# Attention's first two units in another order of issue, and copies of row maxima placed behind the exponentials

## The chip, the core and the metric

The kernel runs on one NeuronCore of a Trainium2 chip, in one launch. The metric is the device time of that launch in microseconds (us); lower is better. The engines are named as the profile names them: PE is TensorE (matmuls), DVE is VectorE, ACT is ScalarE, POOL is GpSimd, SP is SyncE, whose queue here only issues DMAs. Each engine runs its own instructions in the order in which the program holds them, and waits at an instruction whose inputs are not there.

## What is computed

Three layers follow each other: causal attention with a cumulative decay, a mixture of experts, and a gated two-layer net with a short convolution. The change touches the first alone:

```python
B, H, S, D = 4, 8, 576, 64
scores = q @ k.transpose(0, 1, 3, 2) / np.sqrt(D)
cum = np.cumsum(np.maximum(s, 0.0), axis=-1)
bias = -(cum[:, :, :, None] - cum[:, :, None, :])
scores = np.where(causal, -1000000000.0, scores + np.minimum(bias, 0.0))
scores = scores - np.max(scores, axis=-1, keepdims=True)
attn = np.exp(scores)
attn = attn / (np.sum(attn, axis=-1, keepdims=True) + 1e-09)
out = np.matmul(attn, v)
```

## The kernel before

The 32 pairs of batch and head are worked in eight units of four heads each; unit u is half of batch u // 2. A sequence has 576 = 512 + 64 positions; the last 64, the tail, are kept for all heads together in the buffers T1 and T2.

**Operands.** q and k of a unit are loaded as float32 (`load`, L164), scaled and split into two float16 numbers, a high and a low one: ScalarE writes the high part (`split_hi`, L258), VectorE (units 0 and 1) or GpSimd (units 2 to 7) subtracts it from the number to get the low part (`split_lo`, L265). Both parts are then transposed, so that the head dimension lies on partitions: for unit 0 and the tail by matmuls with a unit matrix (`turned`, L299), for the other units by DMA transposes that SyncE issues (`turn`, L278). The result is U[u, 2] (k2 in the program); `copy` (L287) brings its high part into U[u, 1], one of three buffers K1 that the units take in turn. The rows above row 63 of K1 hold what is added to the scores: rows 64 to 69 the decay in three float16 numbers (`extra`, for unit 0 `extra_first`, for the tail `extra_tail`), row 127 of the q half the maximum of the row. For that, the unit's scores are computed once ahead in float16 (`stage_a`: 14 pieces, unit 0 has 15, into PSUM tiles za), VectorE reduces each piece to its maxima (L389, L417), TensorE turns the maxima into rows (`max_turn`, L454), ScalarE copies them out of PSUM (`max_out`, L459; tile mr), and a DMA of `max_row` (L466, for the tail L469) writes them into row 127. Only then may the unit's scores proper start, since they subtract the maximum within the matmul.

**Steps.** A step is one PSUM tile z of 512 scores: `scores` (L488, L491, L516) at step t, the exponentials on ScalarE (`weights`, L527, L532, L533) one step later, the low part on VectorE (`rest`, L544) two steps later, the product with v (`values`, L560) four steps later. A unit has 14 steps. Everything else is placed by hand: a task is planned at a step, with a fraction that orders the tasks of one step, and `work(t)` issues them ahead of the step's scores. The tables in PAR hold these places; those of `start` below zero are issued ahead of step 0. So what matters is the order on each engine:

```python
plan(t0 + c["mx"] + 1, lambda u=u: max_turn(u))
plan(t0 + c["mx"] + 1, lambda u=u: max_out(u))
plan(t0 + c["mx"] + 2, lambda u=u: max_row(u))
```

**SyncE's queue** carries nearly all loads, transposes and rows in one order. With unit 1's row 127 the order is: unit 1's four transposes (two of k, two of q), its decay rows (`extra`), a block of zeros for the output, k and q of unit 3 (L169), k of unit 4 into the buffer that unit 2's k has left, the second half of the first batch's v (L179, L183), unit 2's two transposes, its decay rows, and unit 1's row of maxima. Names of `start` that the steps speak of: `ldq1`, `lk2`, `lq2` are loads; `hk1`, `hq1`, `lk1`, `lq1` the splits of unit 1; `tlk`, `tlq` those of the tail; `T1k`, `T1q` unit 1's transposes; `x1` its decay rows; `xt` the tail's; `mt..`, `mo..`, `mr..` are max_turn, max_out and max_row of unit 0's halves (a, b) and of the tail (t); `pa` to `pd` and `pt` its pieces; `sv0` the split of v.

Of the kernel before, what the change touches and what calls it, by code (L numbers as in the profile page):

```python
# [9 lines left out]
F32 = mybir.dt.float32  # L10
# [16 lines left out]
NH = 4  # L27
# [18 lines left out]
class Keep:  # L46
# [6 lines left out]
PAR = {'u1': {'sv': -3, 'pa': -6, 'pn': 4, 'mx': -3},  # L53
 'u2': {'at': (-22, -21, -19, -18.9, -18), 'cp': (-14, -13), 'lv': -11, 'sv': -2, 'pa': -12, 'pn': 7, 'mx': -6},
# [25 lines left out]
           'wm': -28,  # L80
           'pa': -27,
# [3 lines left out]
           'ldq1': -23,  # L85
           'pb': -22,
           'pc': -21,
           'pd': -20,
           'mtb': -19,
           'thq': -18,  # L90
           'hk1': -17,
           'mob': -16,
           'mrb': -15,
           'lk2': -14,
           'lq2': -13,
           'tlk': -12,
           'tlq': -11,
           'lk1': -10,
           'xt': -9,
           'T1k': -8,  # L100
           'ttk': 2.0,
           'ttq': 3.0,
           'hq1': 3.05,
           'lq1': 3.06,
           'T1q': 3.07,
           'x1': 3.08,
           'ct': 4.0,
           'pt': 4.1,
           'c2': 4.5,
           'sv0': 4.6,  # L110
           'mtt': 5.0,
           'mot': 5.1,
           'mrt': 5.2,
           'z': 6.0,
           'lv1': 8.5},
# [8 lines left out]
def attention(tc, ctx, q, k, v, s, xd, rt, hook):  # L124
# [140 lines left out]
    def split_lo(u, n):  # L265
        i = AT[n]
        a, h = U[u, n].rearrange("p h c (t d) -> p (h c t) d", t=2), U[u, "h"][:, i]
        if u < 2:
            V.scalar_tensor_tensor(h[:, :, i], in0=a, scalar=scale[n], in1=h[:, :, 1 - i], op0=ALU.mult, op1=ALU.subtract)
        else:  # L270
            G.tensor_scalar(a, a, scale[n], 0.0, op0=ALU.mult, op1=ALU.add)
            G.tensor_tensor(h[:, :, i], a, h[:, :, 1 - i], op=ALU.subtract)
# [47 lines left out]
    def extra_first(j):  # L320
        for r, n in ((64, 0), (67, 1)):
            for e in range(2):
                Q.dma_start(K1[0][r + j:r + j + 1, e, n].rearrange("o (h c) -> o h c", h=NH), cp[0:NH, j, 256 * e:256 * e + 256])
# [5 lines left out]
    def copy_tail():  # L329
        for i in range(2):  # L330
            V.tensor_copy(T1[0:64, :, i], T2[64 - 64 * i:128 - 64 * i, :, i])
# [44 lines left out]
    def stage_a(u, halves=False):  # L376
# [14 lines left out]
        def piece(i, hs):  # L391

            n, m = 128 * i + 128, len(hs)
            z = aps.tile([128, 512], F32, name="za")
# [61 lines left out]
    def max_out(u, hs=slice(0, 4), tails=True):  # L456
        n = span(hs, tails).stop - span(hs, tails).start
        mr = U[u, "mr", key(hs)] = wk.tile([18, 128], F16, name="mr")
        A.activation(mr[0:n], U[u, "mt"][0:n, 0:128], AF.Copy, scale=2.0 ** -12)  # L459
# [201 lines left out]
    todo, pieces, copies = {}, {}, {6: [(1, "k")], 7: [(1, "q")]}  # L661

    def plan(t, f):
        todo.setdefault(math.floor(t), []).append((t, len(todo), f))

    def work(t):
        for x in sorted(todo.get(t, ()), key=lambda x: x[0]):
            x[2]()
# [9 lines left out]
    def second_a(r):  # L678
# [12 lines left out]
        xt=extra_tail, ct=copy_tail, ldq1=lambda: load(1, "q"), lk2=lambda: load(2, "k"), lq2=lambda: load(2, "q"),  # L691
# [14 lines left out]
    for u in range(1, NU):  # L706
# [17 lines left out]
        plan(t0 + c["mx"] + 1, lambda u=u: max_out(u))  # L724
# [4 lines left out]
    for t in range(N + 9):  # L729
# [5 lines left out]
        work(t)  # L735
# [9 lines left out]
        if at(2):  # L745
            rest(at(2))
        for d, f in ((4, values), (5, norm), (6, xout)):
            y = at(d)
            if y and y[2] == (3 if y[1] % 2 else 2):
                f(y[0], y[1])  # L750
# [761 lines left out]
def attn_moe_moe2(tc, q, k, v, s, wg, wl, w1, w2, w_in, conv, w_out, out):  # L1512
    nc = tc.nc
    w_in, conv, w_out = (t.bitcast(I32) for t in (w_in, conv, w_out))
    with tc.manual_schedule(), ExitStack() as ctx:
# [13 lines left out]
        def hook(t):  # L1529
# [17 lines left out]
            if PAR["h"]["rc"] <= t < PAR["h"]["rc"] + 80:  # L1547
                for x in range(PAR["h"]["rk"] if t > PAR["h"]["rc"] else 1):
                    next(lay.steps[0], None)
                if t >= PAR["h"]["rc"] + 3:  # L1550
                    next(lay.steps[1], None)
# [98 lines left out]
```

## Time and profile before

| what | us |
|---|---|
| median of three runs | 699.95 |
| lowest and highest of the three | 696.01, 701.78 |
| the profiled execution | 697.92 |
| its span, first to last instruction | 696.2 |
| busy in that span: PE, DVE, ACT, POOL | 631.4, 447.4, 390.6, 250.6 |

The profile is of one execution. Its timeline lists instructions by start, in us from the start of the span, with their duration; equal ones that follow each other are put together with a count. In brackets stands the idle time of the engine ahead of an instruction and what ended it. A list of waits adds such idle times up. The granted clock is a share of TensorE's full 2.4 GHz.

### The profile page before, as it was taken

To read this page: it belongs to the slowest core of one execution; us is meant where nothing else is said; L and a number is where in the kernel's file an instruction comes from. 1 tells how busy PE (TensorE), PEld (TensorE's weight loads), DVE (VectorE), ACT (ScalarE), POOL (GpSimd) and SP (SyncE) were. 2 spreads that over 40 slices of the span, in tenths; PEclk is the share of its full clock that TensorE was granted. 3 is DMA by queue.
4 is the path that set the end of the run, shared out by engine and by line. 5 is a ranking of instruction groups with operands and counts; after the bars stand their busy time and mean duration, and the time that the engine had idled before them with its cause. 6 is when DMAs were issued, how large, how long until landed. Compare 5 with 4: busy or idle time off the path is not lost. (4 is left out here: it accounts for less than half of the span.)

```text
span 696.2 us, 15401 instructions
## 1 busy us (share of the span) xinstructions
PE 631.4 (91%) x5176; PEld 393.5 (57%) x5176; DVE 447.4 (64%) x860; ACT 390.6 (56%) x660; POOL 250.6 (36%) x363
## 2 busy tenths in 40 slices
PE   5675989899999579989999999999599999999997
PEld 2344778688888434434444444444277766665443
DVE  6876688988866696585768586662049984645000
ACT  5553677787788737474746373532059974545111
POOL 8658866654441059812634434342100000000000
PEclk9988899999999769999999999999799999999999
DMA  5876886756646446999999999762390210000111
GB/s 123 189 165 94 145 168 106 169 100 117 183 157 209 129 163 166 296 313 280 248 344 233 325 186 252 180 156 64 69 167 6 46 40 31 16 31 31 45 52 54
DMA packets 168827, 101.81 MB, mean 146 GB/s; under 512 B 119712, under 2 KB 147016, under 8 KB 168732
## 3 DMA queue, kind: packets, MB, share of 16 engines
q1 hardware_dynamic: 164744, 88.65, 53.0%
q0 software_dynamic: 3984, 11.99, 5.5%
q8 instruction: 47, 0.77, 0.5%
q14 instruction: 48, 0.39, 0.2%
q10 hardware_dynamic: 4, 0.00, 0.0%
HBM read 62.18 MB, written 15.31 MB: 111 GB/s over the span
## 5 line engine op out<-in xcount | busy, mean ns | idle before, releaser
L1216 PE MATMUL hp<-r,xt 128*128 x504 | 113.9, 383 | 4.9 <-ACT xt L1247 4.9
L1216 PE MATMUL yp<-r,ht 128*128 x504 | 112.2, 379 | 1.3 <-PEq L1329 1.3
L1484 PE MATMUL o<-wo,g 128*128 128x512 f16 x432 | 94.5, 379 | 0.0
L1436 PEld LDWEIGHTS <-wi 128*128 128x128 f16 x768 | 76.2, 99 | 25.7 <-SPq L1403 4.1
L1216 PEld LDWEIGHTS <-xt 128*128 128x128 f16 x504 | 49.5, 99 | 65.6 <-ACT xt L1247 6.5
L1216 PEld LDWEIGHTS <-ht 128*128 128x128 f16 x504 | 48.5, 98 | 57.0 <-issue 2.3
L1158 DVE SCALAR_TENSOR_TENSOR r<-st,r 128x512 f32 (+3 forms) x80 | 68.3, 914 | 8.8 <-ACT r L1147 7.0
L1436 PE MATMUL hp<-yt,wi 128*128 128x288 f16 x576 | 71.9, 286 | 0.0
L1484 PEld LDWEIGHTS <-g 128*128 128x128 f16 x432 | 42.3, 98 | 49.5
L1147 ACT ACTIVATE r<-st 128x512 f32 (+3 forms) x84 | 57.4, 761 | 21.5 <-SPq L1209 14.6
L1279 POOL DMA_INDIRECT yd<-ys,idx x21 | 21.9, 1041 | 127.1 <-DVEq L1200 63.8
L389 DVE TENSOR_REDUCE mx<-za 128x1 f32<-128x384 f32 (+4 forms) x97 | 56.8, 602 | 14.4 <-PE za L386 13.6
L532 ACT ACTIVATE phi<-z,lnes 128x512 f16<-128x512 f32 (+1 forms) x80 | 50.6, 633 | 24.5 <-PE z L491 22.1
L488 PE MATMUL z<-k 128*128 128x128 f16 (+2 forms) x320 | 50.2, 281 | 9.7 <-DMA k<-mr 5.9
L544 DVE TENSOR_TENSOR plo<-z,phi 128x512 f16<-128x512 f32 (+1 forms) x80 | 48.2, 603 | 13.4 <-ACT z L533 8.7
L533 ACT ACTIVATE z<-z,lnes 128x512 f32<-128x512 f32 (+1 forms) x80 | 48.6, 607 | 0.0
L1453 DVE SCALAR_TENSOR_TENSOR c<-hb,cw,c 128x576 f32<-128x576 f32 x32 | 26.1, 815 | 34.6 <-ACT c L1447 34.6
L1487 ACT ACTIVATE s<-o 128x512 f32<-128x512 f32 x18 | 10.7, 597 | 61.5 <-PE o L1484 61.4
L560 PE MATMUL o<-v,p 128*128 128x65 f32 x256 | 45.0, 287 | 0.0
L1441 ACT ACTIVATE hb<-hp 128x576 f32<-128x576 f32 x32 | 20.5, 642 | 37.9 <-PE hp L1436 37.9
L560 PE MATMUL o<-vv,phi 128*128 128x65 f16 (+1 forms) x512 | 41.6, 202 | 0.0
L1277 ACT ACTIVATE ys<-yp,pp 128x512 f16<-128x512 f32 x21 | 14.3, 683 | 48.4 <-PE yp L1216 34.7
(291 smaller groups left out, 1224.6 us busy)
## 6 DMA issues: line engine op xcount, KB each, us to landing
st<-in_moe_w_dram SPq DMA_DIRECT2D x8, 2048.0 KB
st<-in_moe_w_dram SPq DMA_DIRECT2D x24, 512.0 KB
out_dram<-s SPq DMA_DIRECT2D x18, 256.0 KB
st<-in_k_dram SPq DMA_DIRECT2D x16, 256.0 KB
st<-in_q_dram SPq DMA_DIRECT2D x16, 256.0 KB
xd<-xh SPq DMA_DIRECT2D x16, 256.0 KB
k<-in_moe_w_dram SPq DMA_DIRECT2D x8, 512.0 KB
s<-in_moe_w_in_dram SPq DMA_DIRECT2D x16, 256.0 KB
```

Of the source, the lines that this page charges most:

```text
L389: return lambda: V.tensor_reduce(out, z.rearrange("p (e c) -> p e c", e=m), axis=AX.X, op=ALU.max)
L488: PE.matmul(out, lhsT=ks[i], rhs=qs[i], start=first and not i, stop=False, skip_group_check=True)
L532: A.activation(hi[:, 0:n], z[:, 0:n], AF.Exp, bias=lnes, scale=1.0 / SC)
L533: A.activation(p[:, 0:n], z[:, 0:n], AF.Exp, bias=lnes, scale=1.0 / SC)
L544: (V if md == "a" else G).tensor_tensor(lo[:, 0:n], p[:, 0:n], hi[:, 0:n], op=ALU.subtract)
L560: PE.matmul(out, lhsT=w, rhs=x, start=first, stop=last, skip_group_check=True)
L1147: i = self.nc.scalar.activation(hi, src, AF.Copy, scale=self.scale[w])
L1158: i = nc.vector.scalar_tensor_tensor(lo, in0=src, scalar=sc, in1=hi, op0=ALU.mult, op1=ALU.subtract)
L1216: i = self.nc.tensor.matmul(out, lhsT=lhsT, rhs=self.rings[w][:, c, k, bass.ds(s, 1), f], **kw)
L1436: PE.matmul(st[x][:, n, 0:HN], lhsT=wi[:, c, k, m], rhs=t[:, n, a + k], start=k + a + c == 0, stop=k == 3 and a == 4)
L1453: V.scalar_tensor_tensor(c, in0=h[:, 1:S + 1], scalar=cw[:, m, 1:2], in1=c, op0=ALU.mult, op1=ALU.add)
L1484: PE.matmul(o, lhsT=g[:, a, k, 128 * i:128 * i + 128], rhs=wo[:, c, k], start=j == 0, stop=j == 23)
```

## The change

It has five parts. (1) The start: the last four of the twelve DMAs that write unit 0's decay rows go to GpSimd's queue; the loads of unit 1's q and the tail's decay rows come sooner on SyncE; the subtraction of unit 1's q goes from VectorE to GpSimd; the tail's two copies are made one by VectorE and one by ScalarE, each as soon as its half is turned; unit 0's last two pieces of maxima, their transpose and row go behind the first scores. (2) Every third piece of unit 0's maxima takes its PSUM tile from the pool of z. (3) Unit 1's operands and pieces come one step sooner (`copies`, `pa`, `mx`), and so do unit 2's splits. (4) `work` is called twice a step: tasks with a fraction above 0.75 are issued behind the step's scores, exponentials and subtraction; `max_out` of units 1 to 7 is among these. (5) The splits of the router's weights (L1550) start six steps later. The order of what SyncE issues from unit 1's transposes on is not changed.

The diff, without the table of the start, whose effect the rows of the orders below show:

```diff
@@ -50,8 +50,8 @@
 
 
 
-PAR = {'u1': {'sv': -3, 'pa': -6, 'pn': 4, 'mx': -3},
- 'u2': {'at': (-22, -21, -19, -18.9, -18), 'cp': (-14, -13), 'lv': -11, 'sv': -2, 'pa': -12, 'pn': 7, 'mx': -6},
+PAR = {'u1': {'sv': -3, 'pa': -7, 'pn': 4, 'mx': -4},
+ 'u2': {'at': (-22.5, -21.5, -19, -18.9, -18), 'cp': (-14, -13), 'lv': -11, 'sv': -2, 'pa': -12, 'pn': 7, 'mx': -6},
  'u3': {'load': -35, 'loadq': 0, 'at': (-33, -30, -28, -27, -26.9), 'cp': (-22, -21), 'sv': -1, 'pa': -20, 'pn': 14, 'mx': -6},
  'u': {'load': -51,
        'loadq': 8,
@@ -265,7 +266,7 @@
     def split_lo(u, n):
         i = AT[n]
         a, h = U[u, n].rearrange("p h c (t d) -> p (h c t) d", t=2), U[u, "h"][:, i]
-        if u < 2:
+        if u < 2 and (u, n) != (1, "q"):
             V.scalar_tensor_tensor(h[:, :, i], in0=a, scalar=scale[n], in1=h[:, :, 1 - i], op0=ALU.mult, op1=ALU.subtract)
         else:
             G.tensor_scalar(a, a, scale[n], 0.0, op0=ALU.mult, op1=ALU.add)
@@ -320,15 +321,19 @@
     def extra_first(j):
         for r, n in ((64, 0), (67, 1)):
             for e in range(2):
-                Q.dma_start(K1[0][r + j:r + j + 1, e, n].rearrange("o (h c) -> o h c", h=NH), cp[0:NH, j, 256 * e:256 * e + 256])
+                (G if j == 2 else Q).dma_start(K1[0][r + j:r + j + 1, e, n].rearrange("o (h c) -> o h c", h=NH), cp[0:NH, j, 256 * e:256 * e + 256])
 
     def extra_tail():
         for r, i in ((64, 0), (67, 1)):
             Q.dma_start(T1[r:r + 3, :, i], ext.rearrange("j (b h) c -> j b (h c)", b=B))
 
-    def copy_tail():
-        for i in range(2):
-            V.tensor_copy(T1[0:64, :, i], T2[64 - 64 * i:128 - 64 * i, :, i])
+    def copy_tail(n):
+        i = AT[n]
+        t = T1[0:64, :, i], T2[64 - 64 * i:128 - 64 * i, :, i]
+        if n == "k":
+            V.tensor_copy(*t)
+        else:
+            A.activation(*t, AF.Copy)
 
     def split_v(u):
         b, o = u // 2, u % 2 * NH
@@ -391,7 +396,8 @@
         def piece(i, hs):
 
             n, m = 128 * i + 128, len(hs)
-            z = aps.tile([128, 512], F32, name="za")
+            third = halves and (hs[0] // 2 * 6 + (i if i < 2 else 2 * i - 2 + hs[0] % 2)) % 3 == 2
+            z = zps.tile([128, 512], F32, name="z") if third else aps.tile([128, 512], F32, name="za")
             if halves:
                 busy(z, 1)
             for x, h in enumerate(hs):
@@ -658,14 +664,15 @@
     copy(0, "q")
     load_tail("q")
     load(1, "k")
-    todo, pieces, copies = {}, {}, {6: [(1, "k")], 7: [(1, "q")]}
+    todo, pieces, copies = {}, {}, {5: [(1, "k")], 6: [(1, "q")]}
 
     def plan(t, f):
         todo.setdefault(math.floor(t), []).append((t, len(todo), f))
 
-    def work(t):
+    def work(t, end=None):
         for x in sorted(todo.get(t, ()), key=lambda x: x[0]):
-            x[2]()
+            if end in (None, x[0] - t > 0.75):
+                x[2]()
 
     first, second = slice(0, 2), slice(2, 4)
     P0 = []
@@ -688,7 +695,7 @@
         ttk=lambda: turn_tail("k", range(4), "AVAV"), ttq=lambda: turn_tail("q", range(4), "AVAV"),
         pb=lambda: second_a(range(6, 8)), pc=lambda: second_a(range(8, 10)), pd=lambda: second_a(range(10, 12)),
         mtb=lambda: max_turn(0, second, False), mob=lambda: max_out(0, second, False), mrb=lambda: max_row(0, second, False),
-        xt=extra_tail, ct=copy_tail, ldq1=lambda: load(1, "q"), lk2=lambda: load(2, "k"), lq2=lambda: load(2, "q"),
+        xt=extra_tail, ctk=lambda: copy_tail("k"), ctq=lambda: copy_tail("q"), ldq1=lambda: load(1, "q"), lk2=lambda: load(2, "k"), lq2=lambda: load(2, "q"),
         T1k=lambda: [turn(1, e, slice(0, 1)) for e in range(2)], T1q=lambda: [turn(1, e, slice(1, 2)) for e in range(2)], x1=lambda: extra(1),
         pt=lambda: second_a(range(12, 15)), mtt=lambda: max_turn(0, None), mot=lambda: max_out(0, None), mrt=lambda: max_row(0, None),
         sv0=lambda: split_v(0), lv1=lambda: loadv(0, 1),
@@ -721,7 +728,7 @@
         for i in range(14):
             pieces.setdefault(t0 + c["pa"] + i * c["pn"] // 14, []).append((u, i))
         plan(t0 + c["mx"] + 1, lambda u=u: max_turn(u))
-        plan(t0 + c["mx"] + 1, lambda u=u: max_out(u))
+        plan(t0 + c["mx"] + 1.9, lambda u=u: max_out(u))
         plan(t0 + c["mx"] + 2, lambda u=u: max_row(u))
     for t in sorted(x for x in todo if x < 0):
         work(t)
@@ -732,7 +739,7 @@
         for f in am:
             f()
         am = []
-        work(t)
+        work(t, False)
         at = lambda d: steps[t - d] if 0 <= t - d < N else None
         if at(0):
             scores(at(0))
@@ -744,6 +751,7 @@
             weights(at(1))
         if at(2):
             rest(at(2))
+        work(t, True)
         for d, f in ((4, values), (5, norm), (6, xout)):
             y = at(d)
             if y and y[2] == (3 if y[1] % 2 else 2):
@@ -1547,7 +1555,7 @@
             if PAR["h"]["rc"] <= t < PAR["h"]["rc"] + 80:
                 for x in range(PAR["h"]["rk"] if t > PAR["h"]["rc"] else 1):
                     next(lay.steps[0], None)
-                if t >= PAR["h"]["rc"] + 3:
+                if t >= PAR["h"]["rc"] + 9:
                     next(lay.steps[1], None)
             for i in range(4):
                 if t == PAR["h"]["e"][i]:
```

The places where the order moves, line numbers being those of each kernel (before / after: L169 / L170, L281 / L282, L323 / L324, L466 / L472).

SyncE from the decay rows of unit 0 (`k_141<-cp`) to unit 1's transposes. `in_k`, `in_q` are the loads of the tail's halves (32x8x128), then of units 1 and 2; `k_141<-mr` are unit 0's two rows of maxima; `t_144<-ext` the tail's decay rows. Before:

```order
L323 DMA k_141<-cp 1x4x256 x12
L197 DMA k_146<-in_q_dram 32x8x128 x4
L169 DMA st_112<-in_k_dram 128x4x128 x2
L466 DMA k_141<-mr 1x4x128 x2
L169 DMA st_112<-in_q_dram 128x4x128 x2
L466 DMA k_141<-mr 1x4x128 x2
L169 DMA st_111<-in_k_dram 128x4x128 x2
L169 DMA st_112<-in_q_dram 128x4x128 x2
L327 DMA t_144<-ext 3x4x512 x2
L281 DMA_TRANSPOSE k_436<-st_111 128x16x64 x4
```

After:

```order
L324 DMA k_141<-cp 1x4x256 x8
L198 DMA k_146<-in_q_dram 32x8x128 x4
L170 DMA st_112<-in_k_dram 128x4x128 x2
L170 DMA st_112<-in_q_dram 128x4x128 x2
L472 DMA k_141<-mr 1x4x128 x2
L328 DMA t_144<-ext 3x4x512 x2
L170 DMA st_111<-in_k_dram 128x4x128 x2
L170 DMA st_112<-in_q_dram 128x4x128 x2
L472 DMA k_141<-mr 1x4x128 x2
L282 DMA_TRANSPOSE k_480<-st_111 128x16x64 x4
```

Four DMAs are gone from this queue, unit 1's q load and the tail's decay rows have moved up, and the second row of maxima stands right ahead of the transposes.

GpSimd, from the loads of v on; `st_112`, `st_111` and `h` are q or k of units 1 and 2 and their split halves, `k_143` the buffer K1 of unit 2. Before:

```order
L179 DMA nv<-in_v_dram 64x4x64 x8
L183 DMA nvt<-in_v_dram 32x2x64 x4
L209 MEMSET k_143 128x2x512
L209 MEMSET k_143 64x2x512
L209 MEMSET k_143 3x2x512
L341 MEMSET vv 128x16
L342 MEMSET vv 128x16
L341 MEMSET vvt 128x2
L342 MEMSET vvt 128x2
L343 MEMSET v_558 128x4
L354 TENSOR_SCALAR v_558<-nv 128x4x64
L271 TENSOR_SCALAR st_111<-st_111 128x1024
```

After:

```order
L180 DMA nv<-in_v_dram 64x4x64 x8
L184 DMA nvt<-in_v_dram 32x2x64 x4
L272 TENSOR_SCALAR st_112<-st_112 128x1024
L273 TENSOR_TENSOR st_111<-st_112,st_111 128x16x64
L210 MEMSET k_143 128x2x512
L210 MEMSET k_143 64x2x512
L210 MEMSET k_143 3x2x512
L272 TENSOR_SCALAR st_111<-st_111 128x1024
L273 TENSOR_TENSOR h<-st_111,h 128x16x64
```

The subtraction of unit 1's q (two instructions) stands ahead of the zeroing of `k_143`, and unit 2's k ahead of the small pieces of v.

ScalarE, from the copies of the turned tail on; `t_144` is T1, `p_` the weights of a step, `h<-st_111` the high part of unit 2's k, `mr` the tail's maxima. Before:

```order
L305 ACTIVATE t_145<-o 128x4x128 x2
L263 ACTIVATE st_111<-st_112 128x16x64
L527 ACTIVATE p_531<-z,lnes 128x512
L346 ACTIVATE vv<-nv 128x16x64
L346 ACTIVATE vvt<-nvt 128x2x64
L532 ACTIVATE phi<-z,lnes 128x512
L533 ACTIVATE z<-z,lnes 128x512
L459 ACTIVATE mr<-mt 2x128
L469 DMA t_144<-mr 1x2x128
L527 ACTIVATE p_595<-z,lnes 128x512
L263 ACTIVATE h<-st_111 128x16x64
```

After:

```order
L306 ACTIVATE t_145<-o 128x4x128 x2
L336 ACTIVATE t_144<-t_145 64x4x512
L533 ACTIVATE p_538<-z,lnes 128x512
L538 ACTIVATE phi<-z,lnes 128x512
L539 ACTIVATE z<-z,lnes 128x512
L264 ACTIVATE h<-st_111 128x16x64
L533 ACTIVATE p_581<-z,lnes 128x512
L351 ACTIVATE vv<-nv 128x16x64
L351 ACTIVATE vvt<-nvt 128x2x64
L465 ACTIVATE mr<-mt 2x128
```

Unit 2's k has moved ahead of the tail's row and its DMA, behind the new copy into `t_144`; the split of unit 1's q is gone from this place and stands ahead of step 0.

## Rows read from the trace of the kernel before

**Rows 1.** Waits of TensorE over the whole program: us in total, times, longest.

```profile
PE z L488 <- DMA k<-mr: 5.9, 1, 5.9
```

**Rows 2.** Timeline of TensorE, first scores of units 1 and 2.

```profile
67.86 1.01 PE L488 MATMUL z<-k 128*128 128x512 f16 x2 [5.88 <-DMA k<-mr]
...
98.40 0.59 PE L488 MATMUL z<-k 128*128 128x512 f16 x2
```

**Rows 3.** Stretches: length, busy PE, PEld, DVE, ACT, POOL, PEclk, DMA share, GB/s.

```profile
67.80:74.40 6.60, 6.54 (x52) 5.73 (x52) 2.09 (x5) 2.77 (x5) 6.36 (x10) 0.52 0.89 162
74.40:100.00 25.60, 22.08 (x309) 18.61 (x307) 22.30 (x50) 16.62 (x34) 17.37 (x52) 1.00 0.74 137
```

**Rows 4.** Timeline of SyncE's queue, 25 to 67 us: start, length of the issues.

```profile
25.55 1.20 SPq L466 DMA_DIRECT2D k<-mr  x2
...
30.66 7.53 SPq L281 DMA_TRANSPOSE k<-st  x4
...
41.84 1.08 SPq L169 DMA_DIRECT2D st<-in_q_dram  x2
45.77 1.86 SPq L169 DMA_DIRECT2D st<-in_k_dram  x2
...
55.30 8.28 SPq L281 DMA_TRANSPOSE k<-h  x2
...
65.27 1.40 SPq L466 DMA_DIRECT2D k<-mr  x2
```

**Rows 5.** Waits of SyncE's queue, 0 to 70 us.

```profile
SPq L169 <- POOL h L272: 2.8, 1, 2.8
```

**Rows 6.** Timeline of SyncE's queue, the third of unit 1's transposes.

```profile
34.15 1.90 SPq L281 DMA_TRANSPOSE k<-st  x1
```

**Rows 7.** Timeline of GpSimd, 8 to 50 us.

```profile
8.62 1.39 POOL L647 DMA_DIRECT2D ex<-cp  x2 [0.45 <-ACT cp L253]
...
18.93 4.94 POOL L179 DMA_DIRECT2D nv<-in_v_dram  x8
23.81 2.23 POOL L183 DMA_DIRECT2D nvt<-in_v_dram  x4
...
42.49 1.04 POOL L271 TENSOR_SCALAR st<-st 128x1024 f32<-128x1024 f32 x1 [12.65 <-ACT h L263]
43.62 2.12 POOL L272 TENSOR_TENSOR h<-st,h 128x1024 f16<-128x1024 f32 x1
...
47.28 2.12 POOL L272 TENSOR_TENSOR h<-st,h 128x1024 f16<-128x1024 f32 x1
```

**Rows 8.** Timeline of ScalarE, 32 to 60 us.

```profile
32.58 1.07 ACT L346 ACTIVATE vv<-nv 128x1024 f16<-128x1024 f32 x1
33.53 0.32 ACT L346 ACTIVATE vvt<-nvt 128x128 f16<-128x128 f32 x1
33.73 0.69 ACT L532 ACTIVATE phi<-z,lnes 128x512 f16<-128x512 f32 x1
...
41.36 1.05 ACT L263 ACTIVATE h<-st 128x1024 f16<-128x1024 f32 x1
...
58.88 0.27 ACT L459 ACTIVATE mr<-mt 18x128 f16<-18x128 f32 x1 [5.66 <-PE mt L454]
```

**Rows 9.** Timeline of VectorE: unit 1's subtractions, k, then q.

```profile
26.88 1.22 DVE L269 SCALAR_TENSOR_TENSOR st<-st,st 128x1024 f16<-128x1024 f32 x1
...
32.15 1.23 DVE L269 SCALAR_TENSOR_TENSOR st<-st,st 128x1024 f16<-128x1024 f32 x1
```

**Rows 10.** Timeline of SyncE's queue, 91 to 97 us: unit 2's row, a transpose.

```profile
91.60 1.50 SPq L466 DMA_DIRECT2D k<-mr  x2
...
93.79 2.91 SPq L281 DMA_TRANSPOSE k<-h  x1
```

**Rows 11.** Waits of TensorE, 70 to 215 us, the first of five.

```profile
PE za L386 <- DVE mx L389: 2.3, 4, 1.2
```

**Rows 12.** Page, costliest groups: busy, mean ns of one.

```profile
L1279 POOL DMA_INDIRECT yd<-ys,idx x21 | 21.9, 1041 | 127.1 <-DVEq L1200 63.8
```

More of the change, by code (lines that the diff above doesn't have):

```diff
@@ L80 @@
            'wm': -28,
+           'ldq1': -27.5,
            'pa': -27,
@@ L84 @@
            'mr0a': -24,
-           'ldq1': -23,
            'pb': -22,
            'pc': -21,
-           'pd': -20,
-           'mtb': -19,
            'thq': -18,
            'hk1': -17,
-           'mob': -16,
-           'mrb': -15,
+           'hq1': -16,
+           'xt': -15,
            'lk2': -14,
            'lq2': -13,
[L96 to L100, printed above, removed]
+           'pd': 1.0,
+           'mtb': 1.1,
+           'tlk': 1.2,
+           'lk1': 1.3,
+           'lq1': 1.4,
+           'tlq': 1.5,
+           'mob': 1.8,
+           'mrb': 1.9,
            'ttk': 2.0,
+           'T1k': 2.1,
+           'ctk': 2.8,
            'ttq': 3.0,
[L103 to L113, printed above, removed]
+           'T1q': 3.1,
+           'x1': 3.2,
+           'ctq': 3.3,
+           'c2': 3.5,
+           'pt': 4.8,
+           'mtt': 5.8,
+           'sv0': 5.85,
+           'mot': 5.9,
+           'mrt': 5.95,
            'z': 6.0,
-           'lv1': 8.5},
+           'lv1': 7.5},
  'r': {'cut': 12, 'w1': 6, 'w2': 8, 'w3': 5},
```

## The prediction

> **What bounds the kernel now.** I read the waits of TensorE first. The longest single one of the whole program is a wait for a DMA: matmul L488 waits 5.9 us for a row of maxima [rows 1]. The timeline of TensorE puts it at 67.86 us [rows 2]: after unit 0's last scores the engine stands idle 5.88 us, from 61.98, until unit 1's first scores may start, because row 127 of unit 1's operand has not landed. The stretch behind it runs at a granted clock of 0.52, next to the lower level of 1.2 GHz, up to 74.4 us, and from there at 1.00 [rows 3]. From 70 to 215 us the longest sum of TensorE waits is 2.3 us on VectorE, and no DMA is in that list [rows 11]: behind unit 1's start TensorE is near full, so what its start gains should stay to the end.
>
> What makes the row late is not its computation. ScalarE had copied the maxima at 58.88 + 0.27 = 59.15 us [rows 8], but SyncE issued the row at 65.27 [rows 4]. SyncE works in order and had no rest: from 45.77 it issued unit 4's k, unit 1's values, unit 2's two transposes (55.30, 8.28 us for two), unit 2's extra rows, and then the row, finished at 66.67; the first matmul came 1.19 us later. In front of 45.77 SyncE stood still from 41.84 + 1.08 = 42.92, 2.85 us, for unit 2's k to be given free: the list of SyncE's waits names GpSimd's subtraction L272 with 2.8 us [rows 5]. And in front of that it issued unit 1's four transposes, 30.66 to 38.19, the third (first of q) at 34.15 [rows 4, 6]. So unit 1's start hangs on a chain of issues, and two places in it can move: the start of unit 1's q transposes, and the 2.85 us gap.
>
> **The change part by part.** The order of SyncE's instructions behind unit 1's transposes is the same in both kernels: unit 1's row still stands behind unit 2's two transposes, whatever the change is called. Only the front is another.
>
> *Unit 1's q transposes.* Their input now needs a subtraction on GpSimd in place of one on VectorE (1.23 us at 32.15, [rows 9]). On GpSimd it stands behind the loads of v, whose last issue ended at 23.81 + 2.23 = 26.04 [rows 7], and four DMAs of the decay rows move onto that queue ahead of them. No row shows these four on GpSimd; its 12 issues of v took 4.94 + 2.23 = 7.17 us, 0.60 each, so I take 4 x 0.6 = 2.4 us (below it, nothing: the engine was waiting only 0.45 us there; above it, 1.04 us each as the indirect DMAs of L1279, [rows 12], 4.2 us). The subtraction is two instructions, 42.49 to 43.62 + 2.12 = 45.74, 3.25 us [rows 7]. So 26.04 + 2.4 + 3.25 = 31.7 us, and ScalarE's half of the split is ready well before, since the loads of unit 1's q are issued ahead of both rows of unit 0. The k transposes must be through by then: VectorE's half of k ended at 26.88 + 1.22 = 28.10 and one instruction of that size now stands behind it instead of ahead, so 26.9; the row issued ahead of them ended at 25.55 + 1.20 = 26.75 [rows 4, 9]. Two issues took 34.15 - 30.66 = 3.5 us, so they end at 30.4, in time. The q transposes start at 31.7 in place of 34.15.
>
> *A wait that is new.* The tail's extra rows now stand third behind the first row of maxima and wait for GpSimd's zeroing of that buffer, which the four DMAs push back by the same 2.4 us. Behind them queue unit 2's loads, the second row and unit 1's transposes. The zeroing ended just ahead of 18.93 [rows 7], so now at 21.4, while the second row isn't due until about 25.5: I cost it at nothing; if it is not hidden, the k transposes have 31.7 - 30.4 = 1.3 us to lose first.
>
> *The gap.* With the q transposes at 31.7, SyncE reaches unit 4's k load at 31.7 + (42.92 - 34.15 = 8.8) = 40.5. That load overwrites unit 2's k, which ScalarE splits and GpSimd then subtracts. ScalarE did its part at 41.36 to 42.41 [rows 8], behind the tail's row and its DMA; now it stands ahead of these, behind one copy that comes from VectorE, and three exponentials. The copy has 2048 elements a partition; 1024 took 1.07 and 128 took 0.32 [rows 8], 0.84 ns an element, so 1.07 + 0.86 = 1.93. VectorE's last cast that the copy needs ended by 32.15 even before [rows 9]. So 32.15 + 1.93 + 3 x 0.69 + 1.05 = 37.2, and GpSimd's 3.25 more give 40.45. The load is free as SyncE reaches it, at 40.5 in place of 45.77. The gap goes, and what is late next is SyncE's own queue.
>
> *From there to unit 1.* From 45.77 to the end of the row's issue at 66.67 were 20.9 us, then 1.19 to the matmul: 40.5 + 20.9 + 1.2 = 62.6. Two conditions lie beside it. Unit 2's transposes, now at 50.0, need data that GpSimd had ready at 47.28 + 2.12 = 49.4 even in the old order [rows 7]; the row is issued from 60.0, and ScalarE had the maxima at 59.15 even in the old order. And unit 0's work on TensorE ended at 61.98 even before. Nothing that the change does to unit 0's computation is therefore needed for the sum, and none of its gains (a third PSUM pool for every third piece of maxima, two copies and a subtraction off VectorE) counts in it: they lengthen TensorE's wait. Gain: 67.86 - 62.6 = 5.2 us.
>
> *The copies of maxima behind exponentials*, units 1 to 7: each comes at most one step's exponentials (2 x 0.69) later. Unit 2's row was issued at 91.60 + 1.50 and, at 1.2 us to land, was there at 94.3, its first scores came at 98.40 [rows 2, 10]: 4 us of room. The exponentials come sooner, but TensorE's waits in rows 11 are for VectorE. I take 0 (from a loss of nothing to a gain of 0.5 us in all).
>
> *The clock.* The idle time ahead of unit 1 shrinks but stays about as long as the distance from unit 0's new end to 62.6; the low stretch behind it stays in my sum.
>
> *Sum.* The profiled execution took 697.92 us, 1.72 more than its span of 696.2. Less 5.2 it is 692.7. The median of the three runs, 699.95, lies 2.03 above the profiled one, so the forecast for such a median is 699.95 - 5.2 = 694.7 us, its own range 693.5 to 696.5 by the pieces above.
>
> **A rule that speaks against it.** GpSimd's 12 issues of v ran at 0.60 us each [rows 7]. The Trainium skill, page "SBUF — State Buffer", section "A bandwidth-pool intuition that's wrong (but worth ruling out)", says that a DMA issued from GpSimd can take about 3.1 us in place of 0.62 when VectorE holds the port that the two share. By that figure, an estimate, four issues would cost 12.4 us, the q transposes would start at 41.7, unit 1 at 72.6, and the time would be 704.7. This trace agrees with the undisturbed figure, and shows no disturbed one. The mechanism as such is the last rival.
>
> **The rivals.** *More than the sum.* Unit 2's two transposes took 8.28 us, while a later one took 2.91 [rows 4, 10]: at 2 x 2.91 the row comes 2.5 us sooner, 7.7 in all, and should unit 0 end close to the row, the low stretch shortens too (6.6 us at 0.52 hold some 3 us). For it: the later transpose is as large. Against: unit 1's four, half as large each, took 7.53 us for the same bytes, so 8 us looks like what the DMAs need. Time: 699.95 - 7.7 = 692.3, with the clock down to 690.
>
> *Nothing moves.* If ScalarE's split of unit 2's k stays behind the tail's row (its copy waits on a later cast, or the exponentials wait on scores), GpSimd releases the buffer near 45 as before, the load goes at 45.8 and the q transposes' gain is swallowed by the gap. For it: three engines have to hand over within 0.1 us of my sum's meeting point; against it: a delay there costs only its own length, up to 5. Time: 699 to 700.
>
> *Slower: GpSimd's queue decides.* The 16 issues on GpSimd ahead of the subtraction may be dearer than 0.60 us, and unit 1's q then waits for them. Unit 1's start lies 62.6 - 31.7 = 30.9 us behind the start of the q transposes, so from 67.86 - 30.9 = 37.0 on, 5.3 us later than in my sum, the change loses. At the 1.04 us of rows 12, 16 issues cost 16.7 in place of 9.6, the subtraction ends at 38.8, unit 1 starts at 69.7: 1.8 us lost, 701.8. For it: the engine is the one with new work; against it: the 12 issues that rows 7 show.
>
> **How the numbers follow.** My forecast has a chance of 0.58, more than the sum 0.22, nothing moves 0.12, slower 0.08. The range 690.0 to 700.5 leaves out the slower rival and some of the spread of the runs, which were 696.01 to 701.78, so that 1% (7 us) is about what a measurement can tell from no change. Faster by over 1% (under 692.95): most of the second case and a sixth of the first, 0.30. Slower by over 1% (over 706.95): the dearest part of the last case, and what I have not thought of, 0.05. Within 1%: 0.65.
>
> **What would show it.** Right: in the new profile unit 1's first L488 starts near 62.6 and still waits for the row's DMA, for 3 to 5 us; the third unit 1 transpose is issued near 31.7; SyncE has no gap ahead of unit 4's k near 40.5; the end of the attention part and of the program move by the same 5 us. Wrong: the subtraction on GpSimd ends after 33; SyncE waits for GpSimd's L272 again; unit 1's wait is gone, which would say that I mis-sized unit 2's transposes; or the start comes sooner and a later stretch is longer by as much.

## The result, and the profile after

Over 15 runs of each kernel in turn the median fell from 698.03 to 691.01 us, ratio 0.9894, 95% interval 0.9872 to 0.9917: faster by 1.06%, or 7.0 us, where 5.2 us were forecast. In the profiled executions the span fell from 696.2 to 688.5 us.

The waits of TensorE, 40 to 62 us, after (in us: total, times, longest), against [rows 1]:

```profile
PE z L522 <- DMA t<-mr: 3.7, 1, 3.7
PE za L391 <- DVE k L290: 2.6, 1, 2.6
PE z L494 <- DMA k<-mr: 1.4, 1, 1.4
```

The wait for unit 1's row is down from 5.88 to 1.40 us. Two waits inside unit 0 are new or longer: for the tail's row, and for VectorE's copies. The timeline of TensorE after, first scores of units 1 and 2, and the router's first product:

```profile
61.43 0.59 PE L494 MATMUL z<-k 128*128 128x512 f16 x2 [1.40 <-DMA k<-mr]
...
89.95 0.59 PE L494 MATMUL z<-k 128*128 128x512 f16 x2
...
228.34 0.84 PE L1020 MATMUL nrp<-unit,znr 128*128 128x128 f16 x5 [1.12 <-DVE znr L998]
```

The router's first product before:

```profile
236.71 0.84 PE L1012 MATMUL nrp<-unit,znr 128*128 128x128 f16 x5 [1.12 <-DVE znr L990]
```

Against [rows 2], unit 1 starts 6.43 us sooner and unit 2 8.45. The router's product is 8.37 sooner, so units 2 to 7 are as long as they were: 236.71 - 98.40 = 138.31 us before, 138.39 after. The part behind the router gives 0.7 us back; waits there differ both ways between the two executions (TensorE's for ScalarE's `xt` 5.6 us after, 4.9 before; for SyncE's queue 1.0 after, 3.2 before), so no cause is named.

The timeline of SyncE's queue after, against [rows 4, 6] (a transpose of unit 1 that began at 25.39 is the first of four; the third stands by itself):

```profile
10.90 1.94 SPq L198 DMA_DIRECT2D k<-in_q_dram  x4
...
23.99 1.30 SPq L472 DMA_DIRECT2D k<-mr  x2
...
30.79 1.24 SPq L282 DMA_TRANSPOSE k<-st  x1
...
37.74 1.08 SPq L170 DMA_DIRECT2D st<-in_q_dram  x2
38.93 1.17 SPq L170 DMA_DIRECT2D st<-in_k_dram  x2
40.14 6.93 SPq L180 DMA_DIRECT2D nv<-in_v_dram  x8
...
49.74 6.91 SPq L282 DMA_TRANSPOSE k<-h  x2
...
58.82 1.41 SPq L472 DMA_DIRECT2D k<-mr  x2
```

The gap ahead of unit 4's k (38.93) is gone. The row's issue ends at 60.23, and the matmul comes 1.20 us behind it, as before. GpSimd and ScalarE after, against [rows 7, 8]:

```profile
8.59 2.29 POOL L324 DMA_DIRECT2D k<-cp  x4 [0.45 <-ACT cp L254]
...
20.03 4.96 POOL L180 DMA_DIRECT2D nv<-in_v_dram  x8
24.93 2.19 POOL L184 DMA_DIRECT2D nvt<-in_v_dram  x4
27.20 1.05 POOL L272 TENSOR_SCALAR st<-st 128x1024 f32<-128x1024 f32 x1
28.33 2.43 POOL L273 TENSOR_TENSOR st<-st,st 128x1024 f16<-128x1024 f32 x1
```

```profile
34.19 1.05 ACT L264 ACTIVATE h<-st 128x1024 f16<-128x1024 f32 x1
...
56.39 0.27 ACT L465 ACTIVATE mr<-mt 18x128 f16<-18x128 f32 x1 [1.86 <-PE mt L460]
```

The stretch from unit 1's first scores to unit 2's, before and then after (columns as in [rows 3]):

```profile
67.86:98.40 30.54, 27.21 (x344) 23.29 (x344) 22.77 (x51) 17.79 (x35) 22.68 (x59) 0.90 0.78 142
```

```profile
61.43:89.95 28.52, 25.70 (x344) 21.72 (x345) 23.46 (x52) 18.39 (x37) 24.04 (x64) 0.94 0.80 147
```

It is 2.0 us shorter at a higher granted clock (0.94, not 0.90); 1.5 us of it is TensorE's busy time, the first column (25.70, not 27.21).

### The profile page after: what moved, and what is told of

Its sections match the earlier page's. It is cut to its first block, busy times and chain, and to the rows that moved or that the text cites. A ratio compares the mean times of both kernels' runs of the same rounds, so it can differ in the third digit from the quotient of the medians.

```text
span 688.5 us, 15407 instructions
## 1 busy us (share of the span) xinstructions
PE 627.0 (91%) x5176; PEld 391.7 (57%) x5176; DVE 447.4 (65%) x858; ACT 393.2 (57%) x661; POOL 254.2 (37%) x369
## 5 line engine op out<-in xcount | busy, mean ns | idle before, releaser
L394 DVE TENSOR_REDUCE mx<-za 128x1 f32<-128x384 f32 (+4 forms) x93 | 54.4, 600 | 15.2 <-PE za L391 14.7
L494 PE MATMUL z<-k 128*128 128x128 f16 (+2 forms) x320 | 48.2, 274 | 5.8 <-DVE plo L550 2.5
```

Source lines behind the costliest of these rows:

```text
L394: return lambda: V.tensor_reduce(out, z.rearrange("p (e c) -> p e c", e=m), axis=AX.X, op=ALU.max)
L494: PE.matmul(out, lhsT=ks[i], rhs=qs[i], start=first and not i, stop=False, skip_group_check=True)
```

## The experiments

Theory A: SyncE's queue sets unit 1's start, and TensorE's idling there costs clock behind it (the 2.0 us). Theory B: the queue alone. Theory C: unit 0's lighter work on VectorE. D and E, of runs 10 and 11, are told there. Ratios are to the kernel before, run beside each; starts and waits are read from one profiled execution of each kernel.

**1. The wait filled.** On the kernel before:

```diff
+        if t == PER:
+            busy(mps.tile([128, 512], F32, name="mt"), 24)
```

> The kernel before with 24 matmuls of 128x512 on a unit matrix, whose result nobody reads, ahead of unit 1's first scores, in the 5.9 us in which TensorE waits for unit 1's row. Theory A (SyncE's queue sets unit 1's start, and the clock that falls in the wait costs more behind it): unit 1's first scores still start near 67.9 us, the granted clock behind them is 1.00 in place of 0.52, unit 2's first scores come 1.5 to 2.5 us sooner after unit 1's than the 30.5 us of before, and the program ends 1.5 to 2.5 us sooner than before. Theory B (the queue alone, the clock behind the wait costs nothing that counts): no change, 0 to 0.3 us. Theory C (the gain comes from unit 0's lighter work on VectorE): no change.

Measured: 697.72 us, ratio 0.9997 (0.9969 to 1.0024). The fill overran, and unit 1 started at 68.65 with no wait for the row. From there:

```profile
68.65:97.60 28.95, 25.69 (x345) 21.72 (x344) 22.17 (x49) 17.91 (x35) 21.92 (x59) 0.94 0.79 144
...
120.00:160.00 40.00, 36.87 (x521) 30.50 (x520) 34.53 (x87) 31.01 (x59) 25.22 (x32) 0.96 0.70 136
```

Unit 1 is 1.6 us shorter, as A wants, but it starts 0.8 us later, a low stretch now lies in 120 to 160 us, where the kernel before has a clock of 1.00, and units 2 to 7 take 139.7 us. No gain is measured; the interval, from 2.2 us less to 1.7 us more, leaves room for the 1.5 us that A wanted.

**2. Unit 2's splits late again.** On the changed kernel, so that the gap can return:

```diff
- 'u2': {'at': (-22.5, -21.5, -19, -18.9, -18),
+ 'u2': {'at': (-22, -21, -19, -18.9, -18),
```

> The changed kernel with unit 2's splits back at their old steps, so that ScalarE's part of unit 2's k stands behind the tail's row and its DMA again. A: ScalarE's part at 38.5 to 39.5, GpSimd free of it at 42.8, SyncE stands still until then ahead of unit 4's k (38.9 in the changed kernel), unit 1 starts near 65.3 in place of 61.4, TensorE waits some 5 us for it and the clock falls: 5 to 6 us slower than the changed kernel, 1 to 2.5 faster than before. B: 3.9 us slower than the changed kernel. C: as the changed kernel, within 0.5 us.

Measured: 695.54 us, ratio 0.9965 (0.9938 to 0.9992): by the ratios 4.9 us of the gain lost. SyncE's queue and its wait, then TensorE:

```profile
38.33 1.12 SPq L170 DMA_DIRECT2D st<-in_q_dram  x2
43.05 0.98 SPq L170 DMA_DIRECT2D st<-in_k_dram  x2
```

```profile
SPq L170 <- POOL h L273: 3.5, 1, 3.5
```

```profile
64.57 1.01 PE L494 MATMUL z<-k 128*128 128x512 f16 x2 [8.74 <-DMA k<-mr]
```

The gap is back, for the same GpSimd instruction as in [rows 5]. Unit 0 ended sooner here, at 64.57 - 8.74 = 55.83, and it didn't matter: the row decides.

**3. Unit 1's q subtracted on VectorE again.** On the changed kernel:

```diff
-        if u < 2 and (u, n) != (1, "q"):
+        if u < 2:
```

> The changed kernel with the subtraction of unit 1's q back on VectorE. A: the q transposes follow the k transposes without the wait for GpSimd (30.8 in the changed kernel), at 30.4; unit 4's k load goes at 38.6, unit 1 starts at 61.0 to 61.5; the time is that of the changed kernel, within 0.5 us. C: VectorE's 1.2 us more are on unit 0's path, 1 to 1.5 us slower than the changed kernel.

Measured: 692.75 us, ratio 0.9923 (0.9895 to 0.9952); unit 1 started at 62.33 us, 0.9 later than in the changed kernel. By the ratios that is 2.0 us slower, though the intervals overlap: nearer to C's 1 to 1.5 than to A's nothing. SyncE's queue and its wait:

```profile
30.36 3.46 SPq L282 DMA_TRANSPOSE k<-st  x2
...
40.41 0.92 SPq L170 DMA_DIRECT2D st<-in_k_dram  x2
```

```profile
SPq L170 <- POOL h L273: 1.6, 1, 1.6
```

The q transposes start at 30.36, sooner than the 30.79 of the changed kernel: there they wait for GpSimd's subtraction, here for nothing. The loss comes later. VectorE is behind with the tail, ScalarE splits unit 2's k at 35.92 (34.19 in the changed kernel), and SyncE stands still for 1.6 us ahead of unit 4's k.

**4. Only the early splits, on the kernel before.**

```diff
- 'u2': {'at': (-22, -21, -19, -18.9, -18),
+ 'u2': {'at': (-23.5, -22.5, -19, -18.9, -18),
```

> The kernel before with one thing of the change: unit 2's splits sooner (there by one and a half steps), so that ScalarE's part of unit 2's k stands ahead of the tail's row. A: SyncE's gap ahead of unit 4's k goes, the load at 43.0 in place of 45.8, unit 1 starts near 65.1; TensorE still waits 3 us or more there and the clock falls: 2.8 us faster than before; should the clock stay up, 4.8. B: 2.8 us faster. C: no change.

Measured: 698.2 us, ratio 0.9995 (0.9963 to 1.0026); unit 1 at 66.79. The queue, and its waits:

```profile
42.83 3.82 SPq L169 DMA_DIRECT2D st<-in_k_dram  x2
```

```profile
SPq L169 <- DMA t<-mr: 2.3, 1, 2.3
```

SyncE reaches unit 4's k without a gap, but between its two DMAs it waits for the DMA of the tail's row, issued late by ScalarE (42.16 us). The two share no data; in the trace both signal the same semaphore, number 106. A wait of 2.3 us takes the place of one of 2.8.

**5. The four decay rows back on SyncE.** On the changed kernel:

```diff
-                (G if j == 2 else Q).dma_start(
+                Q.dma_start(
```

> The changed kernel with the four decay-row DMAs back on SyncE's queue. Theory A (SyncE's queue sets unit 1's start, and the clock falls in a long wait): four issues of about 0.6 us stand ahead of unit 1's transposes again, so these, the row and unit 1's first scores come about 2.4 us later than in the changed kernel, near 63.8 us; the wait for the row grows from 1.4 to about 3.8 us, and the stretch behind it may lose up to 1.7 us more by the clock. Time 693.4 to 695.1 us. Theory B (the queue alone): 2.4 us later at unit 1 and the same 2.4 at unit 2, 693.4 us. Theory C (unit 0's lighter work on VectorE makes the gain): that work is unchanged, so 691 us.

Measured: 696.97 us, ratio 0.9995 (0.9962 to 1.0028). The whole gain is gone, which no theory expected. SyncE's queue:

```profile
6.16 8.61 SPq L324 DMA_DIRECT2D k<-cp  x12
14.80 1.92 SPq L198 DMA_DIRECT2D k<-in_q_dram  x4
...
29.48 7.44 SPq L282 DMA_TRANSPOSE k<-st  x4
...
46.01 0.92 SPq L170 DMA_DIRECT2D st<-in_k_dram  x2
```

TensorE: the first piece of unit 0's maxima in the changed kernel, then in this run that piece, unit 0's first scores, the turned tail and unit 1's first scores:

```profile
13.53 0.27 PE L391 MATMUL za<-k 127*128 127x128 f16 x2 [0.70 <-POOL trik L224]
```

```profile
15.39 0.27 PE L391 MATMUL za<-k 127*128 127x128 f16 x2 [1.56 <-POOL tailk L222]
...
23.87 0.60 PE L494 MATMUL z<-k 128*128 128x512 f16 x2 [2.22 <-DMA k<-mr]
...
33.17 1.01 PE L377 MATMUL z<-id 128*128 128x512 f16 x2 [4.32 <-DVE t L308]
...
67.30 0.59 PE L494 MATMUL z<-k 128*128 128x512 f16 x2
```

Unit 0's own chain is late: its tail is turned 6.3 us later (33.17, not 26.89). Three delays make this up. First, the pieces start 1.9 us later. They multiply rows 0 to 126 of K1, among them the rows that the twelve decay DMAs write, and the last of these is issued up to 14.77 (10.88 in the changed kernel); `tailk`, which the view names, is no input of this matmul. Second, 2.66 us pass from the end of the first row's issue (21.21) to the first scores, not 1.07; why isn't shown. Third, VectorE now meets GpSimd's subtraction of unit 1's q: its three subtractions take 6.17 us (from 26.27 to the next instruction at 32.44), not 3.40 (22.75 to 26.15): 2.8 us more. The last of them in the changed kernel, then the last two in this run and GpSimd's instruction:

```profile
25.01 1.22 DVE L298 SCALAR_TENSOR_TENSOR k<-k,k 128x1024 f16<-128x1024 f32 x1
```

```profile
27.40 2.06 DVE L270 SCALAR_TENSOR_TENSOR st<-st,st 128x1024 f16<-128x1024 f32 x1
29.38 3.14 DVE L298 SCALAR_TENSOR_TENSOR k<-k,k 128x1024 f16<-128x1024 f32 x1
```

```profile
28.47 2.97 POOL L273 TENSOR_TENSOR st<-st,st 128x1024 f16<-128x1024 f32 x1
```

Behind that ScalarE splits unit 2's k at 41.53 (34.19 in the changed kernel), and the gap is back (to 46.01). Unit 1 starts at 67.30 without a wait: the row, issued up to 66.12, and unit 0's end come at the same time here. The tail's q, too, is loaded 3.9 us later (14.80, not 10.90), but ScalarE takes it up at 19.88 only, behind the copy of the first maxima.

**6 and 7. Two parts that the forecast took as nothing**, each undone on the changed kernel:

```diff
-        plan(t0 + c["mx"] + 1.9, lambda u=u: max_out(u))
+        plan(t0 + c["mx"] + 1, lambda u=u: max_out(u))
```

> The changed kernel with the copies of maxima ahead of a step's exponentials again, in units 1 to 7. Theories A and B: nothing, 691 us within the spread, and units 2 to 7 as long as in both kernels, 138.3 to 138.4 us from unit 2's first scores to the router. Theory C, widened to the whole attention part (a part of the 7 us is made by these copies): the stretch from unit 2 on gets longer by 1 us or more, and the time is 692 to 694 us.

```diff
-            third = halves and (
+            third = False and halves and (
```

> The changed kernel with all of unit 0's pieces of maxima back in their own pool of PSUM tiles. Theories A and B: unit 0's work may end up to 1 us later than 60.0 us, but the row lands at 61.4 us all the same and sets unit 1's start; 691 us within the spread. Theory C: unit 0 ends late, past 61.4, and the time grows by 1 to 2 us, 692 to 693 us.

Measured: 690.42 us, ratio 0.9903 (0.9877 to 0.9929), and 691.0 us, 0.9903 (0.9865 to 0.9941). Neither differs from the changed kernel; unit 1 at 61.03 and 61.19. Theory C finds nothing here.

**8. Unit 1's row ahead of unit 2's second transpose**, on the changed kernel:

```diff
- 'u2': {'at': (-22.5, -21.5, -19, -18.9, -18),
+ 'u2': {'at': (-22.5, -21.5, -19, -15.9, -15.8),
```

> The changed kernel with unit 1's row between unit 2's two transposes on SyncE's queue. Theories A and B: SyncE waits for the copy of the maxima, done at 56.7 us, issues the row by 58.1 and it has landed by 59.3, so unit 0's end at 60.0 us sets unit 1's start: 1.4 us sooner, no wait for the row, and the second transpose of unit 2 some 5 us later, with room up to unit 2's pieces. Time 689.6 us; if unit 2's pieces then wait for that transpose, 691 to 693 us. Theory C: the row was not what held unit 1, 691 us.

Measured: 691.88 us, ratio 0.9916 (0.988 to 0.9952). Unit 1 started at 60.59, but SyncE waited 4.6 us ahead of the row (issued at 57.40) and TensorE 2.6 us for VectorE inside unit 1. No gain.

**9. The fill, in the run with late splits**, where the row lands at the same time with or without it:

```diff
+        if t == PER:
+            busy(mps.tile([128, 512], F32, name="mt"), 28)
```

> The run with unit 2's splits late again (unit 1 waited 8.7 us for its row there, started at 64.6 us, and unit 2 followed 30.2 us later), with 28 products of the unit matrix, whose result nothing reads, filling TensorE's wait. Theory A (what TensorE does in the wait sets the clock behind it, and this is 1.5 to 2 us of the 7): unit 1 starts at the same 64.6 to 65 us, the low-clock stretch behind it goes, unit 2 follows after 28.5 to 29.0 us, and the time is 1.5 us less, 694 us. Theory B (a low stretch that is kept away here only comes later): unit 2 sooner, but the router no sooner, 695.5 us.

Measured: 695.15 us, ratio 0.9946 (0.992 to 0.9971). Against the 0.9965 of run 2 that is 1.3 us less (0.4 by the medians), within both intervals, so that the time can't tell A's 1.5 us from B's nothing. The stretch of unit 1:

```profile
63.48:93.75 30.27, 27.00 (x343) 22.70 (x344) 21.73 (x49) 18.15 (x36) 22.57 (x59) 0.89 0.77 136
```

It isn't shorter than in run 2 (30.23 us at 0.91): the clock is low at 80 to 90 us here, at 60 to 72 there. The expected 28.5 to 29.0 didn't come.

**10 and 11. The decay rows on GpSimd alone, and with the early splits**, on the kernel before:

```diff
-                Q.dma_start(
+                (G if j == 2 else Q).dma_start(
```

> The kernel before with one part of the change alone: the last four decay-row DMAs of unit 0 on GpSimd's queue. Theory D (these four carry the gain: they hold up the tail's q load on SyncE, and with it unit 0's own chain): the tail's q load is issued near 11 us in place of 14.8, unit 1's transposes and row come 2 to 4 us sooner, unit 1 starts at 64 to 66 us, time 694 to 696 us. Theory E (they help only together with the new order, as the order before has other waits at the same places): unit 1 at 67 to 68 us, 698 us.

> The kernel before with two parts of the change: the four decay-row DMAs on GpSimd's queue and unit 2's splits sooner. Theory D: front and gap of SyncE's queue both move, so unit 1 starts at 62 to 64 us and the time is 692 to 694 us, most of the change's 7 us. Theory E: the early splits push ScalarE's copy of the tail's maxima back, the queue waits for that row's DMA in place of the gap, as in the run with the early splits alone, and the time stays at 697 to 698 us.

Measured: alone 698.07 us, ratio 1.0003 (0.9975 to 1.003), unit 1 at 66.72; with the splits of run 4 696.57 us, 0.9969 (0.9945 to 0.9994), unit 1 at 63.77. TensorE's first piece of maxima before, then in the run with the decay rows alone:

```profile
15.35 0.27 PE L386 MATMUL za<-k 127*128 127x128 f16 x2 [1.59 <-POOL tailk L228]
```

```profile
13.66 0.27 PE L386 MATMUL za<-k 127*128 127x128 f16 x2 [0.73 <-POOL trik L223]
```

Alone, the four DMAs bring this piece 1.7 us sooner, and by the same 1.7 to 1.8 us both of unit 0's rows and unit 1's transposes (from 28.91), while the tail's q load is 3.4 us sooner (11.41): the chain moves with the decay rows and not, as D had it, with that load. At the gap SyncE waits for GpSimd's L272 again. Together the two move the start by 4.1 us, each by itself by 1.1. The time falls by 2.2 us with both, between D's and E's; the profiled execution, 692.12 us, is the fastest of that run.

**12. Unit 1's row ahead of unit 2's extra rows**, on the changed kernel:

```diff
- 'u2': {'at': (-22.5, -21.5, -19, -18.9, -18),
+ 'u2': {'at': (-22.5, -21.5, -19, -18.9, -15.9),
```

> The changed kernel with unit 1's row one step sooner on SyncE's queue, ahead of unit 2's two extra-row DMAs (2.0 us) instead of behind them. Theory A (the row still sets unit 1's start by 1.4 us, unit 0's end is next): the row is issued at 56.8 to 58.2 us, unit 1 starts at 60.0 to 60.5 with no wait for a DMA, time 689.7 us. Rival (what follows is bound by unit 2's operands, which now come later, or by VectorE): unit 1 sooner by 1 us, unit 2 no sooner, 691 us.

Measured: 690.61 us, ratio 0.9895 (0.9863 to 0.9927). Unit 1 at 60.61, no difference of the time that can be measured.

**13 and 14. Unit 1's copy of k on ScalarE, alone and with the order of run 12:**

```diff
+        if (u, n) == (1, "k"):
+            A.activation(o, s, AF.Copy)
+        else:
+            V.tensor_copy(o, s)
```

> The changed kernel with unit 1's copy of its turned k made by ScalarE in place of VectorE. In the changed kernel VectorE's two copies take 3.94 us beside GpSimd's subtraction, 1.41 us where GpSimd is not subtracting (the run with late splits), and TensorE waits 2.6 us for them. Theory A (the row, landing at 61.4 us, sets unit 1's start): TensorE's wait for the copy shrinks to under 1 us, unit 0 ends 1 to 2 us sooner, the wait for the row grows by as much, and the start and the time stay: 61.4 and 691 us. Theory C (unit 0's chain on TensorE and VectorE sets the time): start at 60 us, time 689.5 us.

> Both together: unit 1's row one step sooner on SyncE's queue (alone it gave a start at 60.6 us and no difference of the time beyond the spread) and unit 1's copy of k on ScalarE. Theory A (the start of unit 1 counts one for one): unit 0 ends at 58 to 59 us, the row lands at 59.5 to 60.0, unit 1 starts at 59.5 to 60.2 us, 1.2 to 1.9 us before the changed kernel, time 689 to 690 us. Rival (what unit 1 gains here is lost at unit 2, whose operands and extra rows come no sooner): unit 2 at 89 to 90 us as in the changed kernel, 691 us.

Measured: alone 691.77 us, ratio 0.9909 (0.9875 to 0.9943); both 689.98 us, 0.9868 (0.9828 to 0.9908). TensorE with the copy alone:

```profile
61.00 1.01 PE L498 MATMUL z<-k 128*128 128x512 f16 x2 [3.00 <-DMA k<-mr]
```

Unit 0 ended 2 us sooner, at 58.0, and the wait for the row grew from 1.40 to 3.00: the row binds. In the profile of both, unit 1 started at 61.84 (SyncE's loads of v took 7.34 us in that execution, and the issue of the row 2.33); its median is the lowest, but the interval holds the changed kernel's 0.9894.

## Why the prediction was right in its sign and short in its size

**Right.** The bound: unit 1's start hangs on SyncE's queue, as runs 2 and 13 show from both sides, as long as the row lands behind unit 0's end; in runs 5 and 8 TensorE had no wait for it. Taking unit 1's starts and the ratios of all kernels run, the time follows the start with a slope of 1.04 and a correlation of 0.93 (a straight line through 16 pairs; each start is from one execution, and some of these lie far from the median, as run 2's with 701.08 us for 695.54): four with a start between 66.7 and 68.7 gained nothing, the others gained as they started sooner. The gap went and the load came without one. The 1.2 us from the row's issue to the matmul held. The new wait for GpSimd's zeroing came, 0.7 us ahead of the tail's rows, and was covered, since q's transposes waited for GpSimd anyway. Copies of maxima and the third pool show no effect (runs 6, 7). The slower rival did not come: the four DMAs took 2.29 us on GpSimd, 0.57 each, against 2.4 forecast.

**Right by luck.** The k transposes ended at 30.37, forecast 30.4, but they began at 25.39, not 26.9, and took 4.98 us, not 3.5: two misses that cancel.

**The step that failed in the sum** is the time at which the front ends, "the q transposes start at 31.7", and with it 40.5 and 62.6. Measured: 30.79, 38.93 and 61.43. Of the 1.2 us, 0.9 came at GpSimd: I pushed its loads of v back by the whole 2.4 us of the four DMAs, from 18.93 to 21.3, and they began at 20.03, since its small operations ahead of them took about 1.1 us less than before (the span of its four `tailq` selects fell from 1.57 to 1.10 us, for one); the subtraction itself, 3.6 us for the 3.25 taken, is counted in that 0.9 and gave 0.3 back. 0.6 came between the third transpose and the load: 8.14 us, not 8.8. From the load to the row's end 21.3 us passed, not 20.9. The measured time lies in the range of the rival "more than the sum", yet not by its first mechanism: unit 2's transposes were shorter, 6.91 us for 8.28 [rows 4], but the loads of v ahead of them took 6.93 for 5.31, and nothing was left. The forecast time missed by 3.7 us, 694.7 for 691.01, and 1.9 of these lie in its base: 699.95 was the median of three runs, that of fifteen is 698.03.

**The term set to 0**, "the low stretch behind it stays in my sum", is the other difference in the traces and the rival's second mechanism: 2.0 us in unit 1. The forecast wanted TensorE to wait 3 to 5 us for the row; it waited 1.40, since unit 0 ended at 60.03, no more than 1.95 us sooner than before. TensorE's busy time in unit 1 is longer the lower its granted clock: 24.4 us at 1.00 (run 3), 25.7 at 0.94, 27.2 at 0.90 (before), 28.5 at 0.84 (run 4). The stretch itself holds other waits too (31.6 us at 0.95 in run 8). But it isn't shown that the shorter wait is what kept the clock up in the end: the two fills measured no gain beyond their intervals, these are wider than the effect, and in their traces the low stretch lay elsewhere. With a start 6.4 us sooner and a median 7.0 us lower (5.8 to 8.9 by the interval), the clock is not needed to explain the time; a share of up to 2 us stays open. The recorded clocks give a share of that size: over 99 executions of the kernel before, the time is 3.3 us less for each 0.01 of mean granted clock (correlation -0.63), and the mean clock was 0.964 there and 0.969 in the changed kernel's fifteen runs, which by that slope, an estimate, is 1.6 us. A correlation is no test: in run 9 the clock was 0.006 above run 2's, and its median was only 0.4 us lower.

**What was right for the wrong reason.** The forecast counted the four decay DMAs as a cost on GpSimd only, and credited the front to the move of q's subtraction. The runs say the reverse. With the subtraction back on VectorE the q transposes start sooner still (30.36, run 3); its place is worth something only later, at the gap. The four DMAs gate unit 0's own pieces of maxima, and with them its rows, which stand ahead of unit 1's transposes on SyncE (run 10: 1.7 us at each). Put back on SyncE, they cost the whole gain (run 5): a late unit 0 also meets GpSimd's subtraction on VectorE, and ScalarE's split of unit 2's k, which frees the buffer for unit 4's k, comes late. That is also why the gap and the front had to move together: the early split alone trades one wait for another (run 4), the DMAs alone meet the gap (run 10), both give 4.1 us of start (run 11). No run takes apart what adds the last 2.3 us of the start. The traces put it at SyncE's order: in run 11 unit 1's transposes start at 28.87, 3.9 us behind the second row, with two loads and the tail's rows in between; in the changed kernel these stand ahead of the row and the transposes start at 25.39.

## What to carry to other kernels

Where an in-order queue has two waits in a row, work out where each piece arrives with both removed, and expect nothing from one alone. For DMAs that are moved off a full queue, count first who needs their data and what stands behind them there, and only then what they cost where they go. Before crediting a low clock to a wait, fill the wait, look where the low stretch goes, and take enough runs for an effect of that size: here two fills left it open.

## What was not expected of the hardware

VectorE's fp16 copies and subtractions slow down beside GpSimd's subtraction. The same copy, 64x2048, before, first apart from it and then beside it, and what GpSimd did meanwhile:

```profile
39.81 0.69 DVE L289 COPY k<-k 64x2048 f16<-64x2048 f16 x1
...
44.18 2.12 DVE L289 COPY k<-k 64x2048 f16<-64x2048 f16 x1
```

```profile
43.62 2.12 POOL L272 TENSOR_TENSOR h<-st,h 128x1024 f16<-128x1024 f32 x1
```

It starts at 44.18, GpSimd's instruction ends at 45.74, and the copy ends 0.56 us after that, about its own time of 0.69. GpSimd's next instruction, which started at 45.72, took 1.48 us where the same one took 1.04 at 42.49 [rows 7]. The changed kernel, then run 2:

```profile
36.79 2.93 DVE L355 SCALAR_TENSOR_TENSOR vv<-nv,vv 128x1024 f16<-128x1024 f32 x1 [1.19 <-ACT vv L351]
...
40.15 3.94 DVE L290 COPY k<-k 64x2048 f16<-64x2048 f16 x2
```

```profile
36.74 1.23 DVE L355 SCALAR_TENSOR_TENSOR vv<-nv,vv 128x1024 f16<-128x1024 f32 x1 [0.24 <-ACT vv L351]
...
38.20 1.41 DVE L290 COPY k<-k 64x2048 f16<-64x2048 f16 x2
```

With GpSimd splitting unit 2 early, VectorE's three instructions take 6.87 us in place of 2.64, and unit 0 ends at 60.0, not 55.8; with one of the copies off VectorE it ends at 58.0 (run 13). The Trainium skill, page "SBUF — State Buffer", section "A bandwidth-pool intuition that's wrong (but worth ruling out)", says that GpSimd and a VectorE operation on two ports don't run at the same time, "one fully blocks"; these rows agree for the copies, while GpSimd's DMAs, of which the section gives 3.1 us, took 0.55 to 0.62 us each on average here. In the changed kernel the row hides this loss; in run 5 the same meeting costs unit 0's chain 2.8 us.
